# An attention and mixture-of-experts kernel: a batch's gating arithmetic on GpSimd, its stages set later, and another order of work within a pair of heads

## The chip, the cores and the metric

The kernel runs on one core of a Trainium2 chip. The metric is the device time of one execution in microseconds; a time given for a kernel is the median of its runs. The core's engines are named as in the profile: PE is TensorE with its matmuls (PEld its weight loads), DVE is VectorE, ACT is ScalarE, POOL is GpSimd, and SP is the engine whose queue issues most DMAs. Each engine works through its own list of instructions in order; an instruction that waits for another engine holds everything behind it on its own.

## What is computed

Attention over 8 batches of 8 heads, 576 tokens, 64 columns a head; scores that lie more than tau under their row's maximum are dropped. The outputs of all heads of a token are its row of x (4,608 rows of 512). A gate takes two of eight experts for each row, and the expert layers run over their rows.

```python
scores = scale * np.matmul(q, k.transpose(0, 1, 3, 2))
thresh = np.max(scores, axis=-1, keepdims=True) - tau
scores = np.where(scores >= thresh, scores, -1000000000.0)
attn = np.exp(scores - np.max(scores, axis=-1, keepdims=True))
attn_out = np.matmul(attn / (np.sum(attn, axis=-1, keepdims=True) + 1e-09), v)
...
logits = x @ w_gate
noise_scale = np.log1p(np.exp(x @ w_noise))
noisy_logits = logits + noise_scale * noise
top2 = np.argpartition(-noisy_logits, 2, axis=1)[:, :2]
...
h = np.maximum(x[mask] @ w1[e], 0.0)
out[mask] += top2_w[mask, k, None] * (h @ w2[e])
```

## The kernel before

The program has two stages. The first, `attention`, takes two heads (a pair) at a time: 32 pairs, four to a batch. The second runs the eight experts; its first gathers and first layers stand within the last two batches of the first stage.

A pair's queries are cut into nine row tiles: eight of 128 rows (four for each of the two heads) and a corner that holds the last 64 rows of both. Its steps are these. `split_q` and `split_k` make a rounded copy of the loaded block on ACT (L200, tiles hiq and hik) and the rest of it on POOL by a subtraction of two operands, 128x640 (L201, loq and lok). `scores` (L241) makes the scores of two tiles (12 matmuls) or of the corner (6) into two score buffers in PSUM, sp0 and sp1. `rowmax` takes such a buffer to SBUF with its row maximum on DVE (L254) and the exponential on ACT (L256), and once per two tiles the threshold on ACT (L260, thr). `mask` (L279, DVE) multiplies the exponentials by the comparison with the threshold; its two tensors, ns and e, both lie in SBUF. `ptile`, `prem` and `pcorner` transpose the result on PE (L290, L305, L316) into one of four PSUM buffers, which ACT empties (L292, L295, L307, L309, L318). `avpiece` and `avrem` multiply by the values (L340), `oev` empties that on ACT (L367), `xlpart` transposes back and multiplies by the gate's weights (L383, L384), and `xev` scales it into xr on DVE (L397) with the sums that `norm` and `invert` prepared (L327, L331, L332).

After a batch's last pair come the gating steps on small tiles, at most 320 columns wide: sums of the heads' parts (`gate_sum`, POOL), the softplus of the noise scale (`gate_abs` on DVE, `gate_exp` on ACT, `gate_soft` on POOL, `gate_inverse` on DVE, `gate_soft2` on POOL), the largest two of eight (`gate_max`, `gate_index`, DVE), their one-hot rows (`gate_hot`, DVE, and `gate_both`, POOL), a prefix count by matmuls (`gate_rank`, PE, L577 and L579), slots (`gate_base`, `gate_slot`, `gate_slot2`), and ten `gate_put` DMAs from POOL's queue, which write each token's number and weight into its slot of the table in DRAM (L624).

No scheduler sets the order. Every step is put in a list with a due time, by `at(g, ...)`, the list is sorted, and the instructions are recorded in that order on their engines. Time counts in units of which a pair has nine, so pair n starts at 9n. The due times of a pair's steps are the table PAIR (LAST for the last pair), the gating's are GATING, counted from the batch's last `xev`, and those of the experts' first steps are START. A step of one pair thus stands between steps of the pair before and of the pair after.

In the tables, `scores=(-1.92, -0.37, 3.30, 4.27, 5.98)` are the corner and the four groups of two tiles, so the corner of the next pair stands at 7.08 on this pair's scale, behind the last group at 5.98.

Of the kernel before, what the change touches and what calls it, by code (L numbers as in the profile page):

```python
# [23 lines left out]
N, DM, E, F = B * S, H * D, 8, 1024  # L24
# [26 lines left out]
    scores=(-1.92, -0.37, 2.95, 4.28, 5.25), rowmax=(-1.42, 1.77, 2.48, 2.96, 3.44, 4.42, 4.44, 6.36, 7.05),  # L51
    mask=(1.53, 3.58, 3.71, 5.27, 6.21, 7.13, 7.68, 7.76, 9.27),
    ptile=(5.83, 5.88, 7.88, 9.38, 9.72, 8.52, 9.17, 9.65, 10.24), pcorner=(4.70,), prem=(10.27,), norm=(11.04,),
    invert=(11.25,), avrem=(11.10,), avpiece=(10.38, 11.53, 11.59, 11.60, 11.05, 11.37, 11.43, 11.61),
    oev=(11.68, 12.89), xlpart=(14.08, 13.17, 13.40), xev=(14.49, 13.65))
# [4 lines left out]
GATING = (0, 2.2, 2.4, 3.6, 5.2, 5.4, (7.6, 8.1, 8.6, 9.1, 9.6), (10.1, 10.6, 11.1, 11.6, 12.1), 12.7, 13.2, 14.8, 15.6, 16.6, 17.8)  # L60
# [8 lines left out]
    raw=(-20, -20, -10), tok=-31, ix=-27, ga=(-27, -25, -23), ba=(-25, -23, -21), la=(-23, -20, -18), ta=(-12, -11, -8),  # L69
# [75 lines left out]
def attention(tc, const, work, psum, state, qk, v, tau, wgn, noise, noise_r, out, x_dram, table, experts):  # L145
# [373 lines left out]
    def gate_soft(b):  # L519
        eng = engine(b)  # L520
        d = gt[b]
        e = d["e"]
        u, c, r = (small([NB, E], F32, n) for n in ("gu", "gc", "gr"))
# [60 lines left out]
    def gate_base(b):  # L584
        eng = engine(b)
        d = gt[b]
        rk = small([NB + 1, E], F32, "rk")
# [3 lines left out]
        d["rk"] = rk  # L591
        s = small([NB], F32, "gs")
        eng.tensor_scalar(s, d["e2"], 1.0, 1e-9, op0=ALU.add, op1=ALU.add)
        d["s"] = s
# [608 lines left out]
```

## Time and profile before

| what | us |
| --- | --- |
| median of three runs | 1472.91 (1469.07 to 1472.91) |
| profiled execution: time, span | 1471.25, 1469.5 |
| busy in the span: PE, DVE, ACT, POOL | 1410.2, 884.9, 695.2, 555.4 |
| attention without its start, 42 to 588 us: PE busy of 546 | 520.28 |
| first expert's start, 588 to 715 us: PE busy of 127 | 115.53 |
| experts, 715 to 1428 us: PE busy of 713 | 712.67 |

PE is the engine to look at: it is busy for 96% of the span. So the question for any change is where PE stands idle or slow, and what it waits for there. The clock that the profile lists beside a stretch (PEclk) is the share of TensorE's full clock that was granted; its two levels here are 2.4 GHz (1.00) and 1.2 GHz (0.50), and a stretch between shows a mean of both.

### The profile page before, as it was taken

What the parts mean: (1) busy time and instruction counts of PE and PEld (TensorE: products, weight loads), DVE (VectorE), ACT (ScalarE), POOL (GpSimd) and SP (SyncE); (2) the same over time, 40 slices, a digit from 0 to 9 for tenths busy, and PEclk for the clock granted to TensorE, in tenths of its full rate; (3) what the DMA queues carried; (4) which work ended last, traced back from release to release, by engine and by line L of the source; (5) the groups of instructions that cost most, each with busy time, mean ns of one, the idle gap of its engine ahead of it and who ended that gap; (6) DMA issues with size and microseconds to landing.
All of it is one profiled execution on the core that took longest, in us unless ns stands there. A gap on an engine that the chain in (4) does not pass through costs nothing. (4 is left out here: it accounts for less than half of the span.)

```text
span 1469.5 us, 25882 instructions
## 1 busy us (share of the span) xinstructions
PE 1410.2 (96%) x9242; PEld 1189.8 (81%) x9242; DVE 884.9 (60%) x2530; ACT 695.2 (47%) x1447; POOL 555.4 (38%) x725
## 2 busy tenths in 40 slices
PE   7999999999999998988999999999999999999996
PEld 5776767676767666876998999989999989989884
DVE  6888888888888888544554344444453543543411
ACT  5897989797979787421222122132232221221210
POOL 1223534443434356554152262352342522531612
PEclk8999999999999999999999999999999999999998
DMA  3234343433332234346566376385375474573422
GB/s 116 78 102 109 97 120 95 114 91 108 95 98 85 57 95 130 82 104 156 157 150 153 84 161 150 88 184 155 76 182 141 110 171 117 128 168 90 68 30 32
DMA packets 154115, 166.31 MB, mean 113 GB/s; under 512 B 58148, under 2 KB 105340, under 8 KB 152960
## 3 DMA queue, kind: packets, MB, share of 16 engines
q1 hardware_dynamic: 126784, 125.21, 29.0%
q0 software_dynamic: 27200, 39.42, 16.4%
q8 instruction: 73, 1.20, 0.4%
q14 instruction: 58, 0.48, 0.1%
HBM read 104.42 MB, written 60.15 MB: 112 GB/s over the span
## 5 line engine op out<-in xcount | busy, mean ns | idle before, releaser
L256 ACT ACTIVATE e<-ns,nm 128x576 f32<-128x576 f32 x288 | 213.1, 771 | 72.6 <-DVE ns L254 64.1
L254 DVE TENSOR_SCALAR_CACHE_REDUCE ns<-sp 128x576 f32<-128x576 f32 x279 | 201.4, 753 | 48.1 <-PE sp L241 45.2
L279 DVE SCALAR_TENSOR_TENSOR p<-ns,thr,e 128x576 f32<-128x576 f32 x256 | 202.3, 828 | 12.1 <-ACT thr L260 11.6
L292 ACT ACTIVATE pt<-tp 128x512 f32<-128x512 f32 x256 | 149.5, 593 | 25.0 <-PE tp L290 23.3
L290 PE MATMUL tp<-ident,p 128*128 128x128 f32 x1024 | 155.7, 290 | 4.5 <-ACT pt L292 2.0
L340 PE MATMUL tp<-pt,vt 128*64 128x256 f32 (+1 forms) x1024 | 159.8, 427 | 0.0
L944 POOL DMA_INDIRECT out<-m_y,ix x54 | 87.9, 1629 | 150.3 <-DVE m_y L983 137.4
L944 POOL DMA_INDIRECT out<-m_y,sx x43 | 67.8, 1576 | 194.7 <-DVE m_y L925 159.7
L290 PEld LDWEIGHTS tp<-ident,p 128*128 128x128 f32 x1024 | 118.0, 148 | 27.9 <-issue 10.5
L241 PE MATMUL sp<-hik,hiq 128*128 128x288 f32 (+1 forms) x558 | 117.8, 347 | 14.9 <-DVE ns L254 14.8
L904 ACT ACTIVATE m_p<-m_tp 128x384 fp32r<-128x384 f32 (+1 forms) x66 | 32.6, 494 | 209.5 <-PE m_tp L902 209.3
L925 DVE TENSOR_SCALAR m_y<-m_sp,gw 128x512 f32<-128x512 f32 (+1 forms) x43 | 32.3, 750 | 149.4 <-PE m_sp L923 149.3
L340 PEld LDWEIGHTS tp<-pt,vt 128*64 128x64 f32 x1024 | 78.2, 140 | 46.4 <-issue 27.7
L201 POOL TENSOR_TENSOR loq<-kq,hiq 128x640 fp32r<-128x640 f32 x31 | 49.8, 1606 | 169.1 <-ACT hiq L200 165.3
L241 PEld LDWEIGHTS sp<-hik,hiq 128*128 128x128 f32 (+1 forms) x558 | 64.6, 186 | 55.0 <-DVE ns L254 20.7
L848 POOL DMA_INDIRECT m_p<-x_rows,sx x71 | 70.2, 989 | 81.8 <-DMA stage<-m_p 54.0
L241 PE MATMUL sp<-lok,hiq 128*128 128x288 f32 (+1 forms) x558 | 99.4, 299 | 0.2
L201 POOL TENSOR_TENSOR lok<-kq,hik 128x640 fp32r<-128x640 f32 x31 | 52.5, 1692 | 123.6 <-ACT hik L200 123.5
L241 PE MATMUL sp<-hik,loq 128*128 128x288 f32 (+1 forms) x558 | 97.3, 295 | 0.0
L904 ACT ACTIVATE m_hik<-m_tp 128x384 fp32r<-128x384 f32 (+1 forms) x11 | 5.6, 506 | 178.6 <-PE m_tp L902 178.6
L624 POOL DMA_INDIRECT slot_table<-pay,sl x80 | 82.0, 1025 | 17.6 <-issue 14.0
L902 PE MATMUL m_tp<-m_pt,m_pt 128*128 128x384 f32 (+1 forms) x396 | 72.1, 340 | 0.0
(346 smaller groups left out, 3499.0 us busy)
## 6 DMA issues: line engine op xcount, KB each, us to landing
m_kq<-w SPq DMA_DIRECT2D x128, 256.0 KB
kq<-qk SPq DMA_DIRECT2D x32, 640.0 KB
stage<-m_p SPq DMA_DIRECT2D x63, 256.0 KB
vt<-v SPq DMA_DIRECT2D x8, 1280.0 KB
out<-zeros SPq DMA_DIRECT2D x19, 512.0 KB
x_rows<-xr SPq DMA_DIRECT2D x32, 256.0 KB
m_zeros<-stage SPq DMA_DIRECT2D x96, 64.0 KB
m_vt<-stage SPq DMA_DIRECT2D x96, 64.0 KB
```

Source lines behind the costliest of these rows:

```text
L201: nc.gpsimd.tensor_tensor(lo, x, hi.bitcast(F32), op=ALU.subtract)
L241: nc.tensor.matmul(sp[s][:, hh, 0:HALF], q_[p, 128 * t:128 * t + 128] if j else q_[:, 512:640], k_[p, k0:k0 + HALF], start=(i == 0), stop= ...
L254: nc.vector.tensor_scalar(ns, sp[:, :, 0:HALF], -1.0 / math.sqrt(D) if n else scale, None, op0=ALU.mult, op1=ALU.min, accum_out=nm)
L256: nc.scalar.activation(e, ns, AF.Exp, bias=nm, scale=-1.0)
L279: nc.vector.scalar_tensor_tensor(p, ns, thr, e, op0=ALU.is_le, op1=ALU.mult, accum_out=ssum[n][:, c:c + 1])
L290: nc.tensor.transpose(tp[:, kt, :], p[:, 128 * kt:128 * kt + 128], ident)
L292: nc.scalar.activation(pt[n][:, s, :, COLS[t]:COLS[t] + 128], tp, AF.Copy)
L340: nc.tensor.matmul(av[n, i][64 * s:64 * s + 64, 0:PIECES[i][1] - PIECES[i][0]], w, x, start=(k == 1), stop=(k == 5))
L624: st = nc.gpsimd.indirect_dma_start(out=table, out_offset=bass.IndirectOffsetOnAxis(ap=d["sl"][0:m, i, c:c + 1], axis=0), in_=d["pay"][0:m ...
L848: self.nc.gpsimd.indirect_dma_start(out=r[0:m], out_offset=None, in_=x, in_offset=bass.IndirectOffsetOnAxis(ap=self.tok[e][2][0:m, t:t + 1 ...
L902: nc.tensor.matmul(ps[:, 0:n], w[:, 128 * c:128 * c + 128], x[:, c, 0:n], start=(i == 0), stop=(i == len(ops) - 1))
L944: st = self.nc.gpsimd.indirect_dma_start(out=out, out_offset=bass.IndirectOffsetOnAxis(ap=idx, axis=0), in_=y, in_offset=None, compute_op= ...
```

## The change

It has three parts. First, arithmetic with two tensor operands leaves DVE for the engine of the batch's gating, which is POOL. In `gate_abs` one instruction on DVE becomes two on POOL. In `gate_hot` two on DVE (an addition and a comparison, 128x10 and 128x80) become four on POOL: a copy, the addition, a subtraction and a comparison with zero; `gate_both` goes into it, with its two on POOL. The copy of the running count, `base`, goes from DVE to POOL. Second, `gate_slot` is parted: the products for the slots come with the sum `gs`, and what needs the reciprocal comes as a step of its own, `gate_pay`. The due times of GATING and of the puts lie later, each stage further behind the one that it needs. Third, PAIR, LAST and a few entries of START have other numbers.

```diff
-    scores=(-1.92, -0.37, 3.30, 4.27, 5.98), rowmax=(-1.42, 1.95, 2.09, 3.33, 3.37, 5.08, 5.21, 6.30, 6.64),
+    scores=(-1.40, -0.31, 1.43, 4.02, 6.18), rowmax=(-1.22, 0.76, 0.81, 2.15, 2.24, 4.04, 4.29, 6.81, 7.01),
...
-    oev=(14.49, 19.23), xlpart=(19.31, 20.92, 22.57), xev=(20.54, 23.30), split_q=(-10.40,), split_k=(-5.20,))
+    oev=(14.87, 15.52), xlpart=(16.22, 17.63, 17.67), xev=(17.32, 19.13), split_q=(-9.73,), split_k=(-4.17,))
...
-GATING = (0, 2.2, 2.4, 3.6, 5.2, 5.4, (7.6, 8.1, 8.6, 9.1, 9.6), (10.1, 10.6, 11.1, 11.6, 12.1), 12.7, 13.2, 14.8, 15.6, 16.6, 17.8)
+GATING = (0, 1.6, 3.2, 4.6, 7.2, 7.3, (10.4, 10.9, 11.4, 11.9, 12.4), (12.9, 13.4, 13.9, 14.4, 14.9), 15.5, 18.6, 19.3, 19.4, 21.2, 21.7)
...
-    raw=(-20, -20, -10), tok=-31, ix=-27, ga=(-27, -25, -23), ba=(-25, -23, -21), la=(-23, -20, -18), ta=(-12, -11, -8),
+    raw=(-20, -20, -10), tok=-28, ix=-25.5, ga=(-25, -23, -21), ba=(-23, -21, -19), la=(-21, -18, -16), ta=(-12, -11, -8),
...
     def gate_abs(b):
+        eng = engine(b)
         d = gt[b]
         z = d["l"][:, :, 8:16]
-        d["ab"] = small([NB, E], F32, "ab")
-        vec.scalar_tensor_tensor(d["ab"], z, -1.0, z, op0=ALU.mult, op1=ALU.max)
+        ab = d["ab"] = small([NB, E], F32, "ab")
+        eng.tensor_scalar(ab, z, 0.0, 2.0, op0=ALU.max, op1=ALU.mult)
+        eng.tensor_tensor(ab, ab, z, op=ALU.subtract)
...
-        vec.tensor_tensor(f, d["ix"][:, :, 0:2], off, op=ALU.add)
-        d["oh"] = small([2 * NB, E], F32, "oh")
-        vec.tensor_tensor(d["oh"], iota8[:, None, :].to_broadcast([128, 2 * NB, E]),
-                          f.rearrange("p k c -> p (k c)")[:, :, None].to_broadcast([128, 2 * NB, E]), op=ALU.is_equal)
-
-    def gate_both(b):
-        eng = engine(b)
-        d = gt[b]
+        eng.tensor_copy(f, d["ix"][:, :, 0:2])
+        eng.tensor_tensor(f, f, off, op=ALU.add)
+        oh = d["oh"] = small([2 * NB, E], F32, "oh")
+        eng.tensor_tensor(oh, iota8[:, None, :].to_broadcast([128, 2 * NB, E]),
+                          f.rearrange("p k c -> p (k c)")[:, :, None].to_broadcast([128, 2 * NB, E]), op=ALU.subtract)
+        eng.tensor_scalar(oh, oh, 0.0, None, op0=ALU.is_equal)
+        o = d["oh"].rearrange("p (k c) e -> p k c e", c=2)
+        eng.tensor_tensor(mb[b % 2][:, 0:NB, :], o[:, :, 0, :], o[:, :, 1, :], op=ALU.add)
...
-        vec.tensor_copy(base, rk[:, NB, :])
...
+        eng.tensor_copy(base, rk[:, NB, :])
...
-                to = x + 18.6 + 0.85 * i
+                to = x + 23.1 + 0.7 * i
```

On DVE, the place of a batch's reciprocal `gr` (`gate_inverse`), in the pair after the batch's last. gr needs gu from POOL; ns is a row maximum's output, p and pr are masks, xr is `xev`. Before:

```order
L510 SCALAR_TENSOR_TENSOR ab0_2654<-lgs0_2574 128x40
L279 SCALAR_TENSOR_TENSOR p_119,ssum0_2441<-ns0_2603,thr1_2605,e0_2607 128x576
L279 SCALAR_TENSOR_TENSOR p_119,ssum0_2441<-ns1_2610,thr1_2605,e1_2612 128x576
L279 SCALAR_TENSOR_TENSOR p_119,ssum0_2441<-ns3_2555,thr0_2549,e3_2557 128x576
L531 RECIPROCAL gr0_2682<-gu0_2680 128x40
L279 SCALAR_TENSOR_TENSOR pr0_2713,ssum1_2712<-ns2_2635,thr2_2637,e2_2639 128x576
```

Now:

```order
L254 TENSOR_SCALAR ns2_2656,nm2_2657<-sp0_2648 128x576
L331 RECIPROCAL ssum2_2241<-ssum2_2241 64x1
L332 RECIPROCAL ssum2_2241<-ssum2_2241 128x9
L397 TENSOR_TENSOR xr0_120<-tp0_2643,ssum2_2241 128x2x160
L279 SCALAR_TENSOR_TENSOR p_119,ssum0_2500<-ns0_2632,thr1_2634,e0_2636 128x576
L532 RECIPROCAL gr0_2597<-gu0_2595 128x40
L279 SCALAR_TENSOR_TENSOR p_119,ssum0_2500<-ns1_2638,thr1_2634,e1_2640 128x576
```

The step `gate_abs` is gone from DVE there, and gr stands among other work than before.

On POOL, the same place: lgs is the sum of the heads' parts, gu and gc belong to the softplus, loq and lok are the rests of the splits. Before:

```order
L503 TENSOR_TENSOR lgs0_2574<-t20_2572 128x80
L201 TENSOR_TENSOR loq1_2649<-kq1_2337,hiq1_2648 128x640
L524 TENSOR_SCALAR gu0_2680<-ge0_2656 128x40
L525 TENSOR_SCALAR gc0_2681<-gu0_2680 128x40
L526 TENSOR_TENSOR gc0_2681<-ge0_2656,gc0_2681 128x40
L537 TENSOR_TENSOR gc0_2681<-gc0_2681,gr0_2682 128x40
```

Now:

```order
L503 TENSOR_TENSOR lgs0_2483<-t20_2481 128x80
L511 TENSOR_SCALAR ab0_2528<-lgs0_2483 128x40
L512 TENSOR_TENSOR ab0_2528<-ab0_2528,lgs0_2483 128x40
L201 TENSOR_TENSOR lok0_2574<-kq0_2062,hik0_2573 128x640
L526 TENSOR_SCALAR gu0_2595<-ge0_2567 128x40
L527 TENSOR_SCALAR gc0_2596<-gu0_2595 128x40
L528 TENSOR_TENSOR gc0_2596<-ge0_2567,gc0_2596 128x40
L201 TENSOR_TENSOR loq1_2673<-kq1_2329,hiq1_2672 128x640
L538 TENSOR_TENSOR gc0_2596<-gc0_2596,gr0_2597 128x40
```

gu and the first two of gc have moved ahead of loq, behind lok; one large subtraction now lies between gu and the first instruction that needs gr.

On POOL again, two pairs later: oh is the one-hot tile, mb what the prefix count on PE reads, dl the difference of the two largest. Before:

```order
L201 TENSOR_TENSOR lok1_2788<-kq1_2337,hik1_2787 128x640
L201 TENSOR_TENSOR loq0_2929<-kq0_2590,hiq0_2928 128x640
L569 TENSOR_TENSOR dl0_2960<-mx0_2797 128x5
L571 TENSOR_TENSOR mb1_137<-oh0_2958 128x40
L593 TENSOR_SCALAR gs0_3028<-e20_3017 128x5
```

Now:

```order
L201 TENSOR_TENSOR lok1_2847<-kq1_2329,hik1_2846 128x640
L561 CAST gf0_2940<-ix0_2801 128x10
L562 TENSOR_TENSOR gf0_2940<-gf0_2940,off_128 128x10
L564 TENSOR_TENSOR oh0_2943<-iota8_126,gf0_2940 128x80
L566 TENSOR_SCALAR oh0_2943<-oh0_2943 128x80
L568 TENSOR_TENSOR mb1_137<-oh0_2943 128x40
L570 TENSOR_TENSOR dl0_2947<-mx0_2800 128x5
L201 TENSOR_TENSOR loq0_2950<-kq0_2591,hiq0_2949 128x640
L589 COPY base_140<-rk0_3077 128x8
```

mb stood behind loq and now stands ahead of it, with the four instructions that make it; on PE the count that reads mb (L577, now L576) stood behind the block of transposes of that pair and now stands behind the scores that follow that block.

## Rows read from the trace of the kernel before

**Rows 1.** Windows of stages: length; busy PE, PEld, DVE, ACT, POOL; clock, DMA share, GB/s

```profile
42.00:588.00 546.00, 520.28 (x4510) 384.50 (x4508) 470.15 (x1431) 461.18 (x982) 227.83 (x337) 0.97 0.34 99
588.00:715.00 127.00, 115.53 (x629) 100.68 (x628) 64.34 (x198) 39.68 (x84) 56.57 (x91) 0.97 0.56 130
715.00:1428.00 713.00, 712.67 (x3796) 659.43 (x3795) 316.93 (x806) 169.55 (x335) 252.72 (x265) 1.00 0.55 126
```

**Rows 2.** Waits in 42 to 588 us: who for whom, total, times, longest

```profile
DVE gr L531 <- POOL gu L524: 15.9, 7, 2.3
...
PE sp L241 <- DVE ns L254: 13.8, 21, 1.7
...
PE tp L577 <- POOL mb L571: 6.7, 7, 1.0
```

**Rows 3.** Timeline of POOL: start, duration, what, idle time ahead of it and releaser

```profile
258.96 0.33 POOL L524 TENSOR_SCALAR gu<-ge 128x40 f32<-128x40 f32 x1
```

**Rows 4.** Timeline of DVE at the same place

```profile
259.33 0.40 DVE L531 RECIPROCAL gr<-gu 128x40 f32<-128x40 f32 x1 [2.27 <-POOL gu L524]
...
260.29 0.75 DVE L254 TENSOR_SCALAR_CACHE_REDUCE ns<-sp 128x576 f32<-128x576 f32 x1
```

**Rows 5.** Timeline of PE, one batch: its two waits

```profile
261.11 0.40 PE L241 MATMUL sp<-hik,hiq 64*128 64x288 f32 x1 [1.18 <-DVE ns L254]
...
278.95 0.18 PE L577 MATMUL tp<-mb,tri 128*128 128x48 bf16 x1 [1.00 <-POOL mb L571]
```

**Rows 6.** Timeline of DVE: a mask at the start, a batch's comparison

```profile
18.12 2.08 DVE L279 SCALAR_TENSOR_TENSOR p<-ns,thr,e 128x576 f32<-128x576 f32 x1
...
276.56 1.48 DVE L562 TENSOR_TENSOR oh<-iota,gf 128x80 f32<-128x80 f32 x1
277.96 0.81 DVE L279 SCALAR_TENSOR_TENSOR pr<-ns,thr,e 128x576 f32<-128x576 f32 x1
```

**Rows 7.** Timeline of POOL at these two places

```profile
17.84 1.74 POOL L201 TENSOR_TENSOR lok<-kq,hik 128x640 fp32r<-128x640 f32 x1 [5.06 <-ACT hik L200]
...
276.40 1.55 POOL L201 TENSOR_TENSOR loq<-kq,hiq 128x640 fp32r<-128x640 f32 x1 [7.50 <-ACT hiq L200]
```

**Rows 8.** Windows of two batches and of 4 us behind a wait, columns as in Rows 1

```profile
189.75:261.11 71.36, 68.29 (x607) 50.68 (x607) 61.91 (x192) 61.27 (x132) 31.25 (x50) 1.00 0.37 102
261.11:333.98 72.87, 69.74 (x606) 51.63 (x606) 62.81 (x192) 61.49 (x132) 30.86 (x50) 0.98 0.36 99
...
281.00:285.00 4.00, 3.82 (x19) 2.36 (x17) 3.31 (x10) 3.74 (x9) 0.28 (x1) 0.57 0.01 4
```

**Rows 9.** Timeline of PE: one group of scores and its successor; two pairs' same group

```profile
229.05 0.40 PE L241 MATMUL sp<-hik,hiq 64*128 64x288 f32 x2
...
230.04 0.76 PE L340 MATMUL tp<-ptr,vt 64*64 64x320 f32 x8
...
233.54 0.40 PE L241 MATMUL sp<-hik,hiq 64*128 64x288 f32 x2
...
250.56 0.40 PE L241 MATMUL sp<-hik,hiq 64*128 64x288 f32 x2
```

**Rows 10.** Timeline of ACT: two exponentials, threshold, rounded copy

```profile
264.29 1.43 ACT L256 ACTIVATE e<-ns,nm 128x576 f32<-128x576 f32 x2
265.62 0.28 ACT L260 ACTIVATE thr<-nm,atau 128x2 f32<-128x2 f32 x1
...
266.28 0.82 ACT L200 ACTIVATE hik<-kq,some 128x640 fp32r<-128x640 f32 x1
```

**Rows 11.** Timeline of POOL (a table write) and of PE's weight loads behind it

```profile
228.10 0.96 POOL L624 DMA_INDIRECT slot_table<-pay,sl  x1 [0.21 <-issue]
...
235.97 0.19 PEld L241 LDWEIGHTS sp<-lok,hiq 128*128 128x128 f32 x1 [0.33 <-POOL spacer L623]
```

**Rows 12.** Timeline of DVE and PE after the last batch

```profile
658.88 0.23 DVE L828 TENSOR_SCALAR ix<-ti,jq 128x14 int32<-128x14 int32 x1 [9.21 <-DMA ti<-slot_table]
...
664.06 1.65 PE L923 MATMUL m_sp<-m_pt,m_p 128*128 128x512 f32 x3 [5.03 <-DVE m_y L925]
```

More of the change, by code (lines that the diff above doesn't have):

```diff
@@ L42 @@
 PAIR = dict(
-    scores=(-1.92, -0.37, 3.30, 4.27, 5.98), rowmax=(-1.42, 1.95, 2.09, 3.33, 3.37, 5.08, 5.21, 6.30, 6.64),
-    mask=(1.85, 3.58, 4.11, 5.05, 5.06, 7.09, 9.10, 8.99, 9.05),
-    ptile=(7.22, 6.78, 10.70, 6.07, 7.59, 12.31, 12.70, 10.22, 10.71), pcorner=(5.58,), prem=(11.03,), norm=(14.52,),
-    invert=(15.23,), avrem=(13.45,), avpiece=(12.87, 13.19, 13.58, 14.04, 13.51, 14.11, 16.71, 17.48),
-    oev=(14.49, 19.23), xlpart=(19.31, 20.92, 22.57), xev=(20.54, 23.30), split_q=(-10.40,), split_k=(-5.20,))
-LAST = dict(
[L51 to L55, printed above, removed]
+    scores=(-1.40, -0.31, 1.43, 4.02, 6.18), rowmax=(-1.22, 0.76, 0.81, 2.15, 2.24, 4.04, 4.29, 6.81, 7.01),
+    mask=(1.68, 2.25, 3.18, 5.46, 6.38, 6.60, 7.77, 8.35, 9.04),
+    ptile=(6.67, 7.79, 9.59, 6.76, 9.46, 8.36, 10.35, 8.73, 11.11), pcorner=(5.04,), prem=(9.71,), norm=(10.66,),
+    invert=(16.80,), avrem=(13.11,), avpiece=(11.27, 12.01, 12.33, 14.41, 13.40, 13.79, 14.05, 14.92),
+    oev=(14.87, 15.52), xlpart=(16.22, 17.63, 17.67), xev=(17.32, 19.13), split_q=(-9.73,), split_k=(-4.17,))
+LAST = dict(
+    scores=(-1.40, -0.31, 1.31, 3.45, 4.28), rowmax=(-1.22, 0.45, 1.08, 2.28, 2.59, 3.73, 3.92, 4.75, 4.81),
+    mask=(1.25, 3.10, 3.49, 4.21, 4.30, 6.57, 6.69, 7.05, 7.44),
+    ptile=(3.47, 3.88, 6.30, 6.63, 6.98, 6.99, 7.21, 7.51, 7.97), pcorner=(4.49,), prem=(8.50,), norm=(12.17,),
+    invert=(13.88,), avrem=(10.32,), avpiece=(9.86, 10.05, 10.83, 10.99, 8.91, 11.29, 12.36, 12.38),
+    oev=(11.26, 12.93), xlpart=(12.83, 13.37, 14.10), xev=(14.73, 14.11))
 MLAG = 2
-GATING = (0, 2.2, 2.4, 3.6, 5.2, 5.4, (7.6, 8.1, 8.6, 9.1, 9.6), (10.1, 10.6, 11.1, 11.6, 12.1), 12.7, 13.2, 14.8, 15.6, 16.6, 17.8)
+GATING = (0, 1.6, 3.2, 4.6, 7.2, 7.3, (10.4, 10.9, 11.4, 11.9, 12.4), (12.9, 13.4, 13.9, 14.4, 14.9), 15.5, 18.6, 19.3, 19.4, 21.2, 21.7)
 PIECES = ((0, 320), (320, 576))
@@ L522, in gate_soft @@
         e = d["e"]
-        u, c, r = (small([NB, E], F32, n) for n in ("gu", "gc", "gr"))
+        u, c, r = d["soft"] = [small([NB, E], F32, n) for n in ("gu", "gc", "gr")]
         eng.tensor_scalar(u, e, 1.0, None, op0=ALU.add)
@@ L586, in gate_base @@
         d = gt[b]
-        rk = small([NB + 1, E], F32, "rk")
+        rk = d["rk"] = small([NB + 1, E], F32, "rk")
         vec.tensor_tensor(rk, d["ps"], base[:, None, :].to_broadcast([128, NB + 1, E]), op=ALU.add)
         done(("rank", b))
-        vec.tensor_copy(base, rk[:, NB, :])
[L591 to L594, printed above, removed]
+        eng.tensor_copy(base, rk[:, NB, :])
     def gate_slot(b):
@@ L598, in gate_slot @@
         d = gt[b]
+        s = small([NB], F32, "gs")
+        eng.tensor_scalar(s, d["e2"], 1.0, 1e-9, op0=ALU.add, op1=ALU.add)
         pr = small([NB, 2, E], F32, "gp")
@@ L602, in gate_slot, with gate_pay @@
             eng.tensor_tensor(pr[:, :, c, :], o[:, :, c, :], d["rk"][:, 0:NB, :], op=ALU.mult)
+        d["s"], d["pr"] = s, pr
+    def gate_pay(b):
+        eng = engine(b)
+        d = gt[b]
         r = small([NB], F32, "gq")
@@ L673, in attention @@
             for i, f in enumerate((gate_sum, gate_abs, gate_exp, gate_soft, gate_inverse, gate_soft2, gate_max,
-                                   gate_index, gate_hot, gate_both, gate_rank, gate_base, gate_slot, gate_slot2)):
+                                   gate_index, gate_hot, gate_rank, gate_base, gate_slot, gate_pay, gate_slot2)):
                 for j, t in enumerate(GATING[i] if f in (gate_max, gate_index) else (GATING[i],)):
```

6 lines of the change are left out of this document (1 added, 5 removed).

## The prediction

> **What bounds the kernel now.** I read the windows by stage first. From 715 us on PE is busy for 712.67 of 713 us at full clock; nothing that this change does to the first stage can speed that up, it only lets it begin earlier. What can be won lies before: in 42 to 588 us PE is idle for 546 - 520.28 = 25.7 us, and the granted clock is 0.97, a loss of at most 0.03 x 546 = 16 us of full-clock time [rows 1]. The waits of that stretch then say where the idle time is: 13.8 us are PE's waits to get a score buffer back from DVE's row maximum, 6.7 us, seven waits of 1.0, are its waits for mb from POOL, and above both stands DVE's own wait for gu, seven times 2.3 us [rows 2]. Seven is the number of batches whose gating falls into this stretch.
>
> The timelines of one batch join these up. gu on POOL ends at 259.29 us, behind a large subtraction [rows 3]; DVE has stood still for 2.27 us for it, with two row maxima queued behind [rows 4], and PE, which needs their buffers, for 1.18 us [rows 5]. Eighteen us later the one-hot comparison, which POOL's mb and then PE wait for, takes 1.48 us on DVE, and PE stands for 1.00 us [rows 5, 6]. That comparison is no long operation: it ends at 278.04, and POOL's large subtraction, which began just ahead of it, ends at 277.95 [rows 7]. The mask at 18.12 shows the same, 2.08 us where the one at 277.96 takes 0.81, behind a subtraction from 17.84 to 19.58 [rows 6, 7]. So an instruction of DVE with two SBUF tensors that comes up behind a two-operand instruction of POOL is held until that ends.
>
> The Trainium skill says as much ("GPSIMD Engine Reference", Key points: GpSimd shares its SBUF interfaces with VectorE, in contention with DVE instructions that have two SBUF inputs), and the two rows agree. By that rule alone every two-operand instruction that goes to POOL is one more that can hold a mask, which speaks against this change; it is the second rival below.
>
> The clock is the other half. In the 4 us behind the wait at 278.95 the granted clock is 0.57, so most of them ran at 1.2 GHz; a batch with such a stretch takes 72.87 us and one without 71.36, a difference of 1.5 [rows 8]. PE had waited 1.00 us just ahead of it, and 1.18 some 17 us earlier.
>
> **The change part by part.** Sums are made against the profiled execution, 1471.25 us, which lies 1.7 us under the median of the runs shown and 2.2 over the lowest. A unit of the due times is 17.02 / 9 = 1.89 us, from two pairs in a row [rows 9].
>
> The wait for gu. The new order puts gu behind lok. lok ends a chain that starts when the scores group at 4.02 has been made, which takes 0.99 us [rows 9]: two row maxima of 0.75 [rows 4], the second exponential at half of 1.43, threshold 0.28, rounded copy 0.82 [rows 10], subtraction 1.74 [rows 7]: 5.1 us. With gu's 0.33 [rows 3] it is ready 6.4 us, or 3.4 units, after 4.02, at 7.4 units. gr is due at 8.63 (19.13 + 0.3 + 7.2, less two pairs). That is 1.2 units, 2.3 us, to spare. DVE's 2.27 us and PE's 1.18 go. What is late next is nl for the maxima: the six instructions behind loq have 3.1 units, and at gu's 0.33 they take 2.0 us, with loq ahead of them at 1.55 [rows 3, 7]: 3.6 of 5.9 us.
>
> The wait for mb. Index to rank was 18.6 - 14.9 = 3.7 units apart in the new numbers, 7.0 us. POOL has six instructions there. Their cost at 80 columns is not in the trace; two of them lie between gu's 0.33 at 40 columns and 1.55 at 640 [rows 3, 7]. I take 0.45, nearest to the first, and 0.2 to 0.4 for the others: 2 us, at most 4.5 with the upper end. It fits; PE's 1.00 goes. The 1.48 us on DVE go too, but they lay beside PE's wait and are not counted again. The addition, `gate_abs` and the copy of base leave DVE with some 0.2 us each, beside PE, and count nothing; on POOL they stand behind nothing that PE needs soon.
>
> The two rows of waits hold 13.8 + 6.7 = 20.5 us [rows 2]. The longest wait, 1.7, is not the gating's: it stands where expert 0's token numbers are unpacked on DVE, and stays. The rest is (20.5 - 1.7) / 7 = 2.7 us a batch; in the last of the seven, where the experts' first steps share the queues, I count half of it. So 20.5 - 1.7 - 1.4 = 17.4 us go.
>
> The clock. Slow stretches follow these waits. Five of the first six batches show one, at 1.5 us each [rows 8], and I add one of the next batch's: 9 us. The bounds are nothing and the 16 us of the stage [rows 1].
>
> The order within a pair. PE does the same matmuls. What it waits for most closely is lok, which the next pair's corner scores need: they are due at 7.60, 3.58 units or 6.8 us after the group at 4.02, and lok is ready 0.99 + 5.1 = 6.1 us after it. So 0.7 us are spare. In the old order such a corner waited for lok once a batch, 0.33 us, behind the table writes on POOL [rows 11]; now seven writes lie between loq and lok too, and the two splits are 5.56 units apart where they were 5.20: a write with its issue takes 1.2 us [rows 11], seven and loq 10, the distance 10.5. Bounds: 0.33 us a pair either way, 31 pairs, 10 us; I take nothing.
>
> What is moved beside it. The large load of a pair's block must wait until the later split has read the buffer; that delays SP's queue by at most 2 us, behind it stand stores of x and of zeros that nobody waits for soon, and ten units remain for the load. Expert 0's first loads come two to three units later and its transposes as before; four units or 7.6 us stay for the last. Both count nothing.
>
> The last batch. Its gating runs beside expert layers, and its table writes end in a load for which DVE waits 9.21 us and then PE 5.03 [rows 12]. Here the chain itself counts: POOL's two instructions for `gate_abs` and four for the one-hot rows replace three shorter steps on DVE. At 0.33 to 0.45 each it grows by 1.5 us (bounds 0.5 and 4), all on PE's path.
>
> The Trainium skill has a rule on that price ("GPSIMD Engine Reference", Engine selection: an elementwise operation on a tile belongs on VectorE, since GpSimd is about twice as slow with two inputs). In the first seven batches the work stands beside PE and the rule costs nothing; in the last one it gives the sign that I took.
>
> Sum: 1471.25 - 17.4 - 9 + 1.5 = 1446.4, say 1447.
>
> **The rivals.** *More than the named waits goes.* A batch of four undisturbed pairs would take 4 x (17.02 - 0.33) = 66.8 us against 71.36 to 72.87 [rows 8, 9, 11]. If all of it came, seven batches would gain 7 x 5 = 35 and the time would be 1438. For it: the waits disturb ACT and PE behind them. Against: part of the difference is the rank's own matmuls.
>
> *POOL holds the masks.* Each pair has two large subtractions, and their places against the masks are new. A mask held once a pair costs 2.08 - 0.81 = 1.27 us [rows 6]; the 0.7 us to spare before lok decides. If the chain of every pair is longer by a full hold that lies in it, PE loses up to 31 x 1.27 = 39 us, some with the clock: 1447 + 39 = 1486, slower than before. For it: the shared path is real, and the chain is the tightest that I found. Against: lok starts behind the third mask of its group by the table, and loq beside row maxima, which read PSUM and ran at 0.75 throughout.
>
> *Half.* The waits shrink but the clock still falls behind what is left, or lok costs 0.3 us a pair: 1447 + 9 = 1456 to 1462.
>
> *It doesn't do what it says.* The stalls move to the next in-order wait, to the maxima or to the reciprocal of gs, at the same price: 1471.
>
> **How the numbers follow.** The forecast, 1441 to 1454: 0.52. More: 0.14. Half: 0.16. Held masks: 0.10. Moved stalls: 0.08. Time 1447. The range takes in More and Half and leaves the last two out: 1437 to 1463. A measurement of this kernel tells 0.3%, 4.4 us, from no change; faster by more than that is 0.52 + 0.14 + 0.16 = 0.82, same 0.08, slower 0.10.
>
> **What would show it.** In the profile after: no wait of DVE for gu and none of PE for mb in 42 to 588 us; PE busy for the same 520 us less the slow stretches, in a stage shorter by about 26; a batch near 68 us; clock 0.99 there. DVE's comparison gone, and masks at 0.81. The wait of PE after the last batch at 6 to 7 us where it was 5.03. The prediction is wrong if corner scores wait for lok in ordinary pairs, or if masks of about 2 us stand there.

## The result, and the profile after

The changed kernel takes 1429.44 us in the median (1427.66 to 1434.49), the one before 1472.73 beside it: a ratio of 0.9717, with an interval of 0.9689 to 0.9746. It is faster by 42 us where 24 were forecast, and the time lies below the range. The profiled execution took 1429.14 us, its span is 1427.4.

The windows of the changed kernel answer to [rows 1] and [rows 8]; the columns are the same. The last line is one batch.

```profile
42.00:546.00 504.00, 496.32 (x4522) 366.66 (x4521) 462.87 (x1411) 463.04 (x985) 268.61 (x384) 1.00 0.37 105
546.00:674.00 128.00, 113.48 (x593) 100.69 (x594) 59.62 (x185) 36.70 (x77) 60.62 (x100) 0.96 0.53 131
674.00:1386.00 712.00, 711.55 (x3787) 657.96 (x3786) 315.70 (x801) 169.39 (x334) 253.18 (x266) 1.00 0.55 126
204.29:271.24 66.95, 66.37 (x608) 49.17 (x606) 61.27 (x188) 61.61 (x132) 36.87 (x57) 1.00 0.38 110
```

The experts' stage is what it was. The gain lies ahead of it: the stretch of 546 us is 504 now, at a clock of 1.00 where it was 0.97. PE's idle time fell from 25.7 to 7.7 us, by 18.0, and its busy time by 24.0. A batch takes 66.95 us where it took 71.36 to 72.87.

The waits in 42 to 546 us show what became of [rows 2]: the waits for gu and mb are gone, those for the row maximum have shrunk from 13.8 to 2.7. DVE's own waits for scores are little changed, 42.3 us before and 37.2 now, and they have become shorter pieces (the first line is the kernel before, in 42 to 588 us).

```profile
DVE ns L254 <- PE sp L241: 42.3, 57, 1.4
```

```profile
DVE ns L254 <- PE sp L241: 37.2, 91, 0.8
...
PE sp L241 <- DVE ns L254: 2.7, 8, 1.1
PE tp L290 <- DVE p L279: 2.1, 6, 0.4
```

Once a batch a mask is held on DVE all the same, behind a subtraction on POOL that came up 0.09 us ahead of it (timelines of DVE, of POOL and of PE):

```profile
186.81 2.11 DVE L279 SCALAR_TENSOR_TENSOR p<-ns,thr,e 128x576 f32<-128x576 f32 x1
...
186.72 1.58 POOL L201 TENSOR_TENSOR lok<-kq,hik 128x640 fp32r<-128x640 f32 x1 [5.37 <-ACT hik L200]
...
193.82 0.63 PE L290 MATMUL tp<-ident,p 128*128 128x128 f32 x4 [0.35 <-DVE p L279]
```

[Rows 6] have 0.81 for a mask that is not held. PE loses 0.35 us some 5 us after that mask's end, on a later mask's result; whether more hangs on it is asked below.

A ledger by pairs is the best view of the rest. The corner's transpose (L316) runs once a pair; from one to the next is a pair's period. The second and the last one of the kernel before, then of the changed one:

```profile
39.03 0.30 PE L316 MATMUL tp<-ident,pr 128*64 128x128 f32 x1
...
588.12 0.30 PE L316 MATMUL tp<-ident,pr 128*64 128x128 f32 x1
```

```profile
35.02 0.30 PE L316 MATMUL tp<-ident,pr 128*64 128x128 f32 x1
...
542.13 0.30 PE L316 MATMUL tp<-ident,pr 128*64 128x128 f32 x1
```

So of 42.1 us of span, 4.0 were won ahead of the second corner and 42.0 in the 30 pairs behind it, and 3.9 were lost behind the last.

### The profile page after: what moved, and what is told of

The parts are those of the page before. It is cut to its first block, busy times and chain, and to the rows that moved or that the text cites. A ratio compares the mean times of both kernels' runs of the same rounds, so it can differ in the third digit from the quotient of the medians.

```text
span 1427.4 us, 25886 instructions
## 1 busy us (share of the span) xinstructions
PE 1384.9 (97%) x9242; PEld 1172.2 (82%) x9242; DVE 873.6 (61%) x2498; ACT 697.0 (49%) x1447; POOL 600.6 (42%) x781
## 5 line engine op out<-in xcount | busy, mean ns | idle before, releaser
L279 DVE SCALAR_TENSOR_TENSOR p<-ns,thr,e 128x576 f32<-128x576 f32 x256 | 211.8, 857 | 0.6 <-ACT thr L260 0.6
L290 PE MATMUL tp<-ident,p 128*128 128x128 f32 x1024 | 145.2, 280 | 5.1 <-DVE p L279 2.1
L340 PE MATMUL tp<-pt,vt 128*64 128x320 f32 (+1 forms) x1024 | 145.7, 415 | 0.0
L292 ACT ACTIVATE pt<-tp 128x512 f32<-128x512 f32 x256 | 138.3, 593 | 1.7 <-PE tp L290 0.9
L290 PEld LDWEIGHTS tp<-ident,p 128*128 128x128 f32 x1024 | 113.3, 141 | 19.4 <-ACT ptr L309 4.4
L340 PEld LDWEIGHTS tp<-pt,vt 128*64 128x64 f32 x1024 | 65.1, 136 | 57.3 <-issue 16.5
L241 PE MATMUL sp<-hik,hiq 128*128 128x288 f32 (+1 forms) x558 | 108.4, 345 | 2.7 <-DVE ns L254 2.7
L241 PE MATMUL sp<-lok,hiq 128*128 128x288 f32 (+1 forms) x558 | 93.3, 295 | 0.3 <-POOL lok L201 0.3
L241 PE MATMUL sp<-hik,loq 128*128 128x288 f32 (+1 forms) x558 | 92.1, 292 | 0.0
L241 PEld LDWEIGHTS sp<-hik,hiq 128*128 128x128 f32 (+1 forms) x558 | 59.0, 185 | 37.5 <-DVE p L279 16.6
```

The source lines that it names most:

```text
L241: nc.tensor.matmul(sp[s][:, hh, 0:HALF], q_[p, 128 * t:128 * t + 128] if j else q_[:, 512:640], k_[p, k0:k0 + HALF], start=(i == 0), stop= ...
L279: nc.vector.scalar_tensor_tensor(p, ns, thr, e, op0=ALU.is_le, op1=ALU.mult, accum_out=ssum[n][:, c:c + 1])
L290: nc.tensor.transpose(tp[:, kt, :], p[:, 128 * kt:128 * kt + 128], ident)
L292: nc.scalar.activation(pt[n][:, s, :, COLS[t]:COLS[t] + 128], tp, AF.Copy)
L340: nc.tensor.matmul(av[n, i][64 * s:64 * s + 64, 0:PIECES[i][1] - PIECES[i][0]], w, x, start=(k == 1), stop=(k == 5))
```

## The experiments

**Which half of the change does it.** Each part was put into the kernel before by itself. First the gating alone: its functions, its due times and its table writes.

```diff
-GATING = (0, 2.2, 2.4, 3.6, 5.2, 5.4, ...
+GATING = (0, 1.6, 3.2, 4.6, 7.2, 7.3, ...
...
-                to = x + 18.6 + 0.85 * i
+                to = x + 23.1 + 0.7 * i
```

> The kernel before with the gating's part of the change alone: arithmetic on GpSimd, the new due times of the stages, the table writes at the same distance behind the last addition as in the changed kernel. PAIR, LAST and START are the old ones. Theory A (a ledger of the two traces, pair by pair: 17.5 us of named waits, 10 to 12 us of slow clock behind them, some 5 us of shorter waits that the records count as busy, and 7 us from the order of a pair, 0.23 in each of 31): all but the last goes here, 1436 to 1442. Theory B (the sum of the prediction: only named waits and 9 us of clock): 1445 to 1449. Theory C (the order within a pair is what removes the waits): above 1460.

1464.54 us, ratio 0.9977 (0.9954 to 1.0001). That is the number of theory C, and A and B were wrong, but it did not come about as C had it: in the 26 pairs from the second corner to the 28th this kernel wins 14.7 us, and behind the last corner it loses 12.3. Part of that loss is made by how the run is put together. START's list `gate` gives the last batch's steps their due times by position; the new functions have `gate_rank` where the old ones have `gate_both`, so with the old list the last batch's rank is due at 9 in place of 10, and PE waits 4.0 us there for mb. Next the same with the new START:

```diff
-    raw=(-20, -20, -10), tok=-31, ix=-27, ga=(-27, -25, -23), ...
+    raw=(-20, -20, -10), tok=-28, ix=-25.5, ga=(-25, -23, -21), ...
```

> The gating's part with the new START, and with the old PAIR and LAST. The gating alone lost 12 us against the kernel before behind the last pair, and won 14.6 in 26 pairs ahead of it. If the old START was what it lost by: 8 to 12 us below the gating alone, ratio to the kernel before 0.989 to 0.992. If the old order within the pair made the last batch late: ratio 0.996 to 0.999 as there.

1456.58 us, ratio 0.9912 (0.9879 to 0.9946), as the first theory had it: behind the last corner it takes 883.7 us where the gating alone took 893.6, and that wait is gone. And the other half, the new PAIR, LAST and START with the old gating:

```diff
-    scores=(-1.92, -0.37, 3.30, 4.27, 5.98), ...
+    scores=(-1.40, -0.31, 1.43, 4.02, 6.18), ...
```

> The other half: the kernel before with the new PAIR, LAST and START, its gating with the old arithmetic, old due times behind the last addition and old distance of the table writes. Theory A: 7 us from fewer changes between kinds of matmuls, and the waits stay, 1460 to 1468; pairs with no gating in them take 16.49 us where they took 16.72. Theory B: 1472 within 3. Theory C: 1430 to 1442, with no slow stretch of the clock.

1453.86 us, ratio 0.9888 (0.9853 to 0.9923): 16 us, more than theory A's 7 and far from C's 30 to 42. The ledgers, in us between corners' transposes:

| stretch | before | gating with START | order alone | changed |
| --- | --- | --- | --- | --- |
| start to 2nd corner | 39.0 | 37.5 | 35.0 | 35.0 |
| 2nd to 28th | 469.0 | 454.2 | 451.1 | 435.3 |
| 28th to 32nd | 80.1 | 81.5 | 79.5 | 71.8 |
| 32nd to the end | 881.4 | 883.7 | 885.3 | 885.3 |

In the 26 pairs the halves win 14.8 and 17.9 us and together 33.7, nearly the sum. In the last four pairs, beside the experts' first steps, neither wins more than 0.6, and both win 8.2. A batch at full clock, of the gating with START and of the order alone (windows, columns as above):

```profile
174.61:244.65 70.04, 67.60 (x607) 50.42 (x607) 61.22 (x188) 61.08 (x133) 33.14 (x56) 1.00 0.37 105
```

```profile
170.08:239.25 69.17, 66.82 (x609) 49.23 (x607) 61.76 (x192) 61.67 (x133) 33.01 (x49) 1.00 0.37 106
```

Against 71.36 that is 1.3 and 2.2 us; both together give 4.4. The waits of PE for mb are gone with either half, and each makes waits of its own: 0.81 and 0.92 us of PE once a batch with the gating and START, 1.70 with the order alone. In the 26 pairs the slow stretches (five before, one with the gating and START, two with the order alone, none in the changed kernel; 1.7 us of lost time each) and 0.25 a pair for the order, worked out below, leave an estimate for the waits alone: 8 us by the gating with START, 6 by the order, 19 by both. The full price of the waits needs both halves.

**The arithmetic itself.**

```diff
-        eng.tensor_scalar(ab, z, 0.0, 2.0, op0=ALU.max, op1=ALU.mult)
-        eng.tensor_tensor(ab, ab, z, op=ALU.subtract)
+        vec.scalar_tensor_tensor(ab, z, -1.0, z, op0=ALU.mult, op1=ALU.max)
...
-        eng.tensor_scalar(oh, oh, 0.0, None, op0=ALU.is_equal)
```

> The changed kernel with the arithmetic of three stages back on VectorE (the absolute value, the one-hot rows up to the comparison, the copy of base), at the new due times. If the later due times are what removes the waits: within 3 us of the changed kernel, 1427 to 1433, with a comparison on DVE that may be held to about 1.5 us but that nobody waits for. If VectorE, busy for 463 of 504 us, has no room for it: seven batches at about 2 us, 1440 to 1445, and PE's waits for the row maxima come back.

1428.22 us, ratio 0.9716 (0.9686 to 0.9746): the changed kernel's time. So at the new due times the engine of the gating's arithmetic, which the change is named after, does nothing for the whole time. (The new arithmetic at the old due times was not run.) The parts differ by a few us that cancel: from the 28th corner to the 32nd this kernel takes 74.1 us, with one slow stretch of 6.8, where the changed one takes 71.8, and from there to the end 882.0 for 885.3. The timelines of DVE and POOL show why the batches before the last are not affected: at its new place the comparison is short, 0.24 where [rows 6] have 1.48, and mb is done 4.3 us before PE comes to it.

```profile
192.15 0.24 DVE L562 TENSOR_TENSOR oh<-iota,gf 128x80 f32<-128x80 f32 x1
...
192.47 0.27 POOL L565 TENSOR_TENSOR mb<-oh 128x40 bf16<-128x40 f32 x1 [4.49 <-DVE oh L562]
```

**The price of one wait.** The rank was set so early that PE comes to it before mb is written.

```diff
-..., 15.5, 18.6, 19.3, 19.4, 21.2, 21.7)
+..., 15.5, 16.2, 19.3, 19.4, 21.2, 21.7)
```

> The changed kernel with one due time altered: rank at 16.2 in place of 18.6 units. PE then comes to the rank's matmuls about 4.4 us sooner, by the trace of the changed kernel about 1.5 us before mb is written. It prices one wait a batch, seven in all. If a wait of this length makes the clock fall behind it as in the kernel before: 7 x (1.5 + 1.5 to 1.7) = 21 to 22 us, 1449 to 1452, with a slow stretch in most batches. If the slow stretches had another cause: 7 x 1.5 = 10 us, 1439 to 1441, clock 1.00. If PE makes up for a wait within the batch: under 4 us.

1455.16 us, ratio 0.9903 (0.9865 to 0.9941): 26 us above the changed kernel for seven waits. PE's timeline in one batch, and the window of a batch at full clock:

```profile
195.10 1.03 PE L290 MATMUL tp<-ident,p 128*128 128x128 f32 x8
197.50 0.18 PE L576 MATMUL tp<-mb,tri 128*128 128x48 bf16 x1 [1.36 <-POOL mb L568]
...
198.10 0.33 PE L383 MATMUL tp<-ident,ot 128*128 128x128 f32 x1 [0.31 <-ACT pt L292]
...
201.47 0.66 PE L290 MATMUL tp<-ident,p 128*128 128x128 f32 x4 [0.25 <-ACT pt L292]
...
202.81 0.66 PE L290 MATMUL tp<-ident,p 128*128 128x128 f32 x4 [0.20 <-ACT pt L292]
```

```profile
134.69:204.00 69.31, 66.55 (x601) 48.64 (x601) 61.55 (x187) 61.33 (x131) 37.55 (x56) 1.00 0.36 106
```

The row says 1.36 us. The batch is 69.31 - 66.95 = 2.36 longer, at full clock. Two things are missing in the row. The modelled end of the eight transposes lies some 0.17 us behind the point at which the next matmul could have started (in the changed kernel that comes 0.87 us after their start, not 1.03). And three short waits for evictions follow, 0.76 us in sum. So six batches make 14 us. Slow stretches came behind three of the six waits, 13.7 us at half speed; their pairs take 22.1, 20.8 and 21.0 us where the other three take 19.8, which is 4.4 us more. The rest is the seventh batch, in the last four pairs, where PE waited 6.5 us: they take 77.9 us for 71.8.

**The order and the blocks.** PE's long matmuls (L340, most with 128x64 weights) stand in blocks between transposes (128x128, the corner's 128x64) and scores (64x128). By its order the kernel before has four blocks in an ordinary pair, the changed one three; two of the three are one run that the corner's transpose cuts in two. Two runs add and remove blocks with the work unchanged.

```diff
-    ..., avpiece=(11.27, 12.01, 12.33, 14.41, 13.40, 13.79, 14.05, 14.92), oev=(14.87, 15.52), ...
+    ..., avpiece=(11.27, 12.01, 12.33, 14.41, 13.40, 13.79, 15.70, 15.80), oev=(14.87, 15.95), ...
```

> The changed kernel with the last two of a pair's eight steps of weights times values set between transposes: avpiece[6:8] at 15.70 and 15.80, the second output eviction at 15.95. The work is the same; PE enters and leaves its long matmuls of L340 five times in a pair in place of three. In the changed kernel a step out of them takes 0.31 to 0.34 us from start to start where one within takes 0.22 on average, and a step into them 0.20 where a transpose follows a transpose in 0.11. If that is what the order within a pair bought (0.23 us a pair): two more blocks at 0.1 to 0.2 each, 31 pairs, 6 to 12 us slower than the changed kernel, 1435 to 1441, and ordinary pairs of 16.7 to 16.9 us at full clock. If the order bought something else: 1427 to 1432, pairs of 16.49.

Ratio 0.9862 (0.9825 to 0.9899), 1468.40 us. The other:

```diff
-    ..., pcorner=(5.04,), ...
+    ..., pcorner=(4.05,), ...
```

> The changed kernel with the corner's transpose (pcorner) at 4.05 in place of 5.04, ahead of the weights times values and no longer in the middle of them: PE has two blocks of L340 in a pair in place of three. If a block costs 0.1 to 0.2: ordinary pairs of 16.3 to 16.4 us, 3 to 6 us less than the changed kernel, 1423 to 1427. If not: 1427 to 1432. If the corner's earlier eviction on ScalarE stands in the way of an exponential: slower than the changed kernel by a few us.

Ratio 0.9690 (0.9658 to 0.9722), 1439.31 us. The chip of these runs needs a word. The kernel before took 1486.38 us on it, and each of the four traces taken there shows stops of DVE of 3 to 6 us, about once a batch, within or behind a run of table writes; here with hik's copy later:

```profile
219.52 0.81 DVE L279 SCALAR_TENSOR_TENSOR p<-ns,thr,e 128x576 f32<-128x576 f32 x1
...
226.10 0.76 DVE L254 TENSOR_SCALAR_CACHE_REDUCE ns<-sp 128x576 f32<-128x576 f32 x1 [5.76 <-PE tp L340]
```

So single pairs without it are compared. Corners' transposes in a row, two blocks (fewer_switches, from its run below), three (the changed kernel), four (the kernel before), five (more_switches):

```profile
49.61 0.30 PE L316 MATMUL tp<-ident,pr 128*64 128x128 f32 x1
65.94 0.30 PE L316 MATMUL tp<-ident,pr 128*64 128x128 f32 x1
```

```profile
51.49 0.30 PE L316 MATMUL tp<-ident,pr 128*64 128x128 f32 x1
67.97 0.30 PE L316 MATMUL tp<-ident,pr 128*64 128x128 f32 x1
```

```profile
72.63 0.30 PE L316 MATMUL tp<-ident,pr 128*64 128x128 f32 x1
89.36 0.30 PE L316 MATMUL tp<-ident,pr 128*64 128x128 f32 x1
```

```profile
69.07 0.30 PE L316 MATMUL tp<-ident,pr 128*64 128x128 f32 x1
86.17 0.30 PE L316 MATMUL tp<-ident,pr 128*64 128x128 f32 x1
```

16.33, 16.48, 16.73 and 17.10 us at full clock. The two runs that move blocks, with the rest of the order as it was, give 0.15 us for a block (two to three) and 0.31 (three to five), the second more than was expected; the kernel before lies between, 0.25 for one block, though its order differs in other things too. That is what the order bought in every pair. The price is that of the step out of L340 and back, from start to start (the changed kernel):

```profile
66.96 1.08 PE L340 MATMUL tp<-pt,vt 128*64 128x256 f32 x8
67.97 0.30 PE L316 MATMUL tp<-ident,pr 128*64 128x128 f32 x1
68.20 1.62 PE L340 MATMUL tp<-pt,vt 128*64 128x256 f32 x12
```

The eight matmuls, two at a time, stand 0.21 to 0.26 us apart; from the last two to the transpose it is 0.31, and 0.23 from there back. The Trainium skill has a rule that seems near ("TensorEngine Tiling (Array Packing)", Key Properties: a change of the tiling mode drains TensorE), but these rows don't bear it out as the cause. The step above stays at 128x64 and costs 0.31 us, the same as a step from L340 to a 128x128 transpose in more_switches. And counted by the shapes in the rows, a pair has 11 changes of shape in the kernel before, 11 in the changed one, 12 in fewer_switches and 15 in more_switches, which is not the order of their times. What makes the step dear is open.

The changed kernel and fewer_switches ran once more, on one chip without the stop.

> The changed kernel itself, on the chip of the three runs beside it. In the runs of the switches and of hik every kernel, the one before among them, took some 14 us more, and VectorE stood still for 4 to 6 us once a batch, where the changed kernel's first trace has no such stop. If the chip makes them: gone on another chip, 1427 to 1434, and back on the same one with 1440 to 1446. If the altered due times make them: never here.

> The kernel with the corner's transpose ahead of the weights times values, once more beside the changed one. By its trace ordinary pairs take 16.32 us in place of 16.49, and the pair with the held mask 16.46 in place of 17.48, since that mask was under way when lok came up. By both: 31 x 0.17 + 7 x 0.85 = 11 us below the changed kernel on the same chip. If the pairs' gain is taken back in the last two pairs, where experts' steps share the queues: 3 to 6 us below.

1429.34 us (0.9734, 0.9700 to 0.9768) and 1420.34 us (0.9661, 0.9627 to 0.9695). The stop was gone for both; fewer_switches is one kernel with it on one chip and without it on another, so the due times don't make it. (No kernel was run a second time on the first chip.) Fewer_switches is 9 us below the changed kernel, and so the fastest of all. The blocks are about half of that, 30 x 0.15 = 4.5 us; the pair with the held mask takes 16.46 us in place of 17.47, since no mask is held there.

**The held masks.** Two runs move the rounded copy of the keys, and with it the subtraction on POOL, against the masks.

```diff
-    ..., split_k=(-4.17,))
+    ..., split_k=(-4.80,))
```

> The changed kernel with the split of the keys at -4.80: on ScalarE hik stands ahead of the second exponential of its group, and lok on GpSimd runs while two or three masks of the same group come up, in every pair. It is the rival of held masks made on purpose. If a hold costs its length on PE (0.9 to 1.3 us a pair): 28 to 39 us more than the changed kernel, 1457 to 1468. If it costs what the one held mask a batch costs there (0.35): 31 x 0.35 = 11 us, 1440. If VectorE's idle time of 0.4 to 0.6 us a group takes it in: under 4 us, 1429 to 1433.

Ratio 0.9783 (0.9743 to 0.9823), 1453.57 us, on the chip with the stop. Here a mask is held in every pair, as at 69.52 (timelines of DVE and POOL, then the corners of PE):

```profile
69.52 1.71 DVE L279 SCALAR_TENSOR_TENSOR p<-ns,thr,e 128x576 f32<-128x576 f32 x1 [0.32 <-ACT thr L260]
...
68.71 1.90 POOL L201 TENSOR_TENSOR lok<-kq,hik 128x640 fp32r<-128x640 f32 x1 [7.33 <-ACT hik L200]
```

```profile
51.36 0.30 PE L316 MATMUL tp<-ident,pr 128*64 128x128 f32 x1
67.87 0.30 PE L316 MATMUL tp<-ident,pr 128*64 128x128 f32 x1
84.39 0.30 PE L316 MATMUL tp<-ident,pr 128*64 128x128 f32 x1
```

An ordinary pair takes 16.51 us, 0.03 more than the changed kernel's, for 0.9 us more on DVE. DVE has that time, by its 37.2 us of waits for scores. The pair with the gating's maxima and indices takes 17.33. The other way:

```diff
-    ..., split_k=(-4.17,))
+    ..., split_k=(-3.95,))
```

> The changed kernel with the split of the keys at -3.95 in place of -4.17: on ScalarE hik then stands behind the corner's two evictions, and lok on GpSimd begins some 0.4 us later. In the changed kernel a mask of 2.10 us stands once a batch behind lok, which began 0.08 us ahead of it; now that mask should be under way when lok comes up, and take 0.81. If the 0.35 us that PE waits once a batch follow from that mask: 6 x 0.35 = 2 us less, 1427. If nothing hangs on it: no change. If lok has no 0.4 us to spare, corner scores wait for it in every pair: 31 x 0.2 to 0.4 = 6 to 12 us more, 1435 to 1441.

Ratio 0.9719 (0.9678 to 0.9760), 1447.64 us, the changed kernel's ratio. But the hold once a batch is gone, and the pair that had it takes 16.63 us where it took 17.48. So the one hold that does cost, costs 0.85: it falls on the pair in which DVE also does the maxima and indices. Six such pairs would be 5 us, which the ratio can't show beside the stops (its interval is 6 us to either side); and the later lok makes PE wait for it 3.0 us, in six waits. In medians on this chip hik's earlier copy lies 5.9 us above the later one, about what seven pairs of 17.33 for 16.63 make. Two more runs ask whether such holds are what either half alone still pays.

```diff
 (gating with START)
-    ..., split_q=(-10.40,), split_k=(-5.20,))
+    ..., split_q=(-7.775,), split_k=(-5.20,))
```

> The gating's part with the new START, old PAIR and LAST, and the split of the queries at -7.775 in place of -10.40 (of the pair it is for): on ScalarE hiq then stands behind one more eviction, and loq on GpSimd begins some 0.5 us later, when the corner's mask is under way. Without the move one such mask a batch takes 2.06 us, PE waits 0.82 and 0.42 behind it, and a batch is 70.05. If the held mask is what this half still pays: the mask at 0.81, a batch of 68.6 to 68.9, and 6 x 1.3 = 8 us below the gating with START, ratio to the kernel before 0.984 to 0.987. If it is VectorE's short instructions for maxima and indices, which stand in the same place: a batch of 69.7 or more, ratio 0.990 to 0.992.

Ratio 0.9878 (0.9853 to 0.9904), 1469.26 us, between the two. The held mask is gone, and its pair takes 17.11 us where it took 18.33; but ordinary pairs take 17.12 where they took 16.72. Undecided.

```diff
 (order alone)
-    ..., split_k=(-4.17,))
+    ..., split_k=(-3.95,))
```

> The order alone, with the split of the keys at -3.95 in place of -4.17: hik stands behind the corner's two evictions, and lok on GpSimd begins some 0.4 us later, when the mask is under way that it now holds for 2.11 us once a batch. If that hold is what the order alone still pays: a batch of 67.8 to 68.3 where it was 69.16, the wait of 1.70 of PE for an eviction of pt gone, 6 x 1.0 to 1.3 = 6 to 8 us, ratio to the kernel before 0.983 to 0.985. If the old gating's own wait for gu (up to 3.0 us on VectorE) is what it pays: a batch of 68.9 or more, ratio 0.988 to 0.990.

Ratio 0.9741 (0.9719 to 0.9762), 1448.19 us. The ratio is lower than either theory's, but not for the theory's reason: the kernel before takes 1485.59 us on this chip, 16 more than beside the order alone, and this kernel does not share the loss. Its profiled run spans 1451.8 us, the order alone's 1450.9. A batch without a slow stretch takes 69.35 us, no less than 69.17, and PE's wait is still there, 1.52. So the hold is not what the order alone pays. Its trace points at mb (POOL, then PE, of the order alone):

```profile
189.15 1.67 POOL L201 TENSOR_TENSOR lok<-kq,hik 128x640 fp32r<-128x640 f32 x1 [8.24 <-ACT hik L200]
190.78 0.71 POOL L569 TENSOR_TENSOR dl<-mx 128x5 f32<-128x5 f32 x1
191.46 0.26 POOL L571 TENSOR_TENSOR mb<-oh 128x40 bf16<-128x40 f32 x1
...
195.81 0.33 PE L383 MATMUL tp<-ident,ot 128*128 128x128 f32 x1 [1.70 <-ACT pt L292]
```

mb stands behind lok, the rank and the corner's scores behind mb, and an eviction on ACT behind the corner's exponential. That chain is read, not tried by itself.

**The ends.**

```diff
 (the changed kernel with the old tables)
-    scores=(-1.40, -0.31, 1.31, 3.45, 4.28), ...
+    scores=(-1.92, -0.37, 2.95, 4.28, 5.25), ...
...
-    raw=(-20, -20, -10), tok=-28, ix=-25.5, ...
+    raw=(-20, -20, -10), tok=-31, ix=-27, ...
```

> The changed kernel with the old LAST and START: the order of the last pair, and the times of the experts' first steps and of the last batch's gating. From the last pair's corner to the end the changed kernel takes 885.3 us, the one before 881.3. If LAST and START cost this: 3 to 4 us below the changed kernel. If it is the longer chain of the last batch's gating on GpSimd (1.5 us by the prediction) and where the clock falls: within 2 us of it. If the new START is needed for the gating's new times: above it by 5 to 10.

1438.28 us, ratio 0.9793 (0.9759 to 0.9827): 9 us above the changed kernel, the third theory. With the old START PE waits 4.3 us for the last batch's mb, a wait that the new one doesn't have: there too the rank is due at 9 in place of 10, as with the gating alone.

## Why the prediction missed, step by step

The sign held, and so did the place of the gain; the sum was 17 us short. The step that failed is "I take nothing" for the order within a pair. From span to span, the 42.0 us of the 30 pairs are 7.5 of order, 13.7 of clock and 21 of waits; 4.0 were won ahead of them and 3.9 lost behind.

**The order within a pair: 0 forecast, 7.5 measured in the 30 pairs.** "PE does the same matmuls" is true, and "I take nothing" does not follow. The price stood in the trace of before: two matmuls of L340, one for each head, follow the last two after 0.21 to 0.26 us, and the first score stands 0.31 to 0.36 behind the last. One block less is 0.25 a pair, 30 x 0.25 = 7.5. The order alone also reaches the second corner as early as the changed kernel, 35.0 us for 39.0; how much of these 4.0 is the order and how much the clock's start the traces don't settle (with the clock's lost time taken off it is 2.3 in the changed kernel and 0.6 in the order alone). The bound of 10 us, meant for lok, nearly held all of it; the value taken did not, since the order was priced by waits alone.

**The waits: 17.4 forecast, about 21 measured.** gu, mb and the row maxima went as computed. The chains were sized well: POOL's six instructions from gf to dl take 2.4 us (2 forecast), and mb is there 4.4 us before PE. PE's idle time fell by 18.0. But the sum took idle times in rows as the whole price, and the early rank shows 2.36 for a row of 1.36. The 42.0 us less the clock and the order leave 20.8; the 2.8 above 18.0 I put down to such tails, by subtraction. And the prediction put all of this on the gating's later times, where the halves show that neither they nor the order wins half of it alone.

**The clock: 9 forecast, 13.7 measured at most.** Five stretches in the first six batches is right, one behind them is too few: in the last four pairs the kernel before has three. From the second corner to the last it has eight of 3.4 us at half speed, the changed one none; its longest wait of PE in 42 to 500 us is 0.36. By pairs a stretch costs 1.5 us (20.42 for 18.95), eight of them 12, and the waits would then be 22.

**The last batch: 1.5 forecast, 3.9 measured, and not where it was named.** From the last corner to the end PE's idle time grew from 11.8 to 15.5 us. The wait named for it, 6 to 7 us in place of [rows 12]'s 5.03, is 4.06. What is new there is another wait, for an expert's tile that POOL reaches only after a run of table writes:

```profile
573.14 0.81 PE L903 MATMUL m_sp<-m_vt,m_pt 128*128 128x384 f32 x2 [4.10 <-POOL m_pt L802]
```

The runs with the arithmetic back on DVE and with the order alone have it too, 4.1 us in both, and the gating with START has not: so it comes with the new order, and not with the arithmetic on POOL, for which the 1.5 was taken. What that arithmetic costs in the last batch is not shown apart: with it back on DVE the kernel takes 3.3 us less from the last corner on, but comes to that corner 2.2 later.

**The rivals.** *More than the named waits goes* came true and was then overtaken. It put a batch at 66.8, and it is 66.95, which is partly luck: the 66.8 were four pairs of the old order, and four new ones take 4 x 16.48 = 65.92, so 1.0 us a batch is still paid. *POOL holds the masks*: the masks of 2 us came, once a batch, so the mark named for it stood in the profile; its price of 1.27 a pair did not. In an ordinary pair a hold costs 0.03, in the pair with the indices 0.85. The 0.7 us that lok had to spare nearly did: in the changed kernel PE waits for lok once in 42 to 546 us, 0.3, in the second run of fewer_switches five times, 0.5 at most. The Trainium skill's rule on this ("GPSIMD Engine Reference", Key points: GpSimd shares SBUF interfaces with DVE instructions that have two SBUF inputs) agrees with the 2.11; that it costs time doesn't follow from it. *Moved stalls* did not come in the whole change; in kind they are seen in its halves, each of which makes a new wait.

## What to carry to other kernels

Before an order is costed at nothing, count how often the bound engine leaves one kind of matmul for another, and price one such step from start-to-start times. A wait's row can be less than its price, as for the early rank: look for the tail of the work ahead of it, the short waits behind it, and the clock. An operation that was held on an engine that waits anyway cost next to nothing here; it cost where that engine had other work.

## What the runs showed of the hardware

A block of L340's matmuls set apart by other matmuls costs 0.15 to 0.31 us in the two runs that move blocks alone, and leaving L340 takes 0.31 us from start to start, also where the weights' shape stays 128x64. The clock fell in five of six batches with waits of PE of 1.18 and 1.00 us (the kernel before), in three of six behind waits of 1.36 (the early rank), in two of six behind waits of 1.70 (the order alone), and in none of them where the longest was 0.36 (the changed kernel): so a longer wait did not make it fall more often. On one chip all four traces show stops of VectorE of 3 to 6 us about once a batch, and the kernel before takes some 14 us more there than elsewhere. On another it is as slow, but the two traces from that one don't show these stops. So kernels from these chips were compared by ratio or by single pairs, and a ratio misleads where only one of two kernels is slowed. What makes either stays open.
